# A hand-written order of work: the second batch's turns, and stages 2 and 3 of later batches, at other places

## The chip, the cores and the metric

The kernel runs on one core of a Trainium2 chip. The metric is the time of one execution on the device in microseconds (us); the median of several executions is compared. The core's engines are TensorE (PE in the profile; its weight loads are PEld), VectorE (DVE), ScalarE (ACT), GpSimd (POOL) and SyncE (SP), which here only issues transfers. Each engine works through its own instructions in the order in which the program gives them.

## The reference

Eight batches of 2496 positions and 256 channels go through a filter in the frequency domain, and each of the 19968 resulting rows then through one of eight experts, which is chosen by a hash of the row's token number.

```python
X = np.fft.rfft(x, axis=1)                       # x: (8, 2496, 256)
Y = X * (filt_r + 1j * filt_i)[None, :, :]
x = np.fft.irfft(Y, n=2496, axis=1).reshape(19968, 256)
expert_idx = token_ids * np.int64(2654435761) % np.int64(8)
for e in range(8):
    mask = expert_idx == e
    h = np.maximum(x[mask] @ w1[e], 0.0)         # w1: (8, 256, 1024)
    out[mask] = h @ w2[e]                        # w2: (8, 1024, 256)
```

All of it is in float32.

## The kernel before

**The filter.** 2496 is split as 39 x 64, and the transform of a batch is done in three stages. Stage 1 (`stage1`, or `stage1_c` for batches 0 and 1) is a transform over 39, with matmuls that write `pa`; stage 2 (`stage2`: `forward` writes `pb`, `back` writes `pc`) a transform over 64, the filter's product (three VectorE lines, 279 to 283, that make `y`) and the way back over 64; stage 3 (`stage3`, matmuls that write `pd`) the way back over 39. A batch has six pieces of stages 1 and 3 (`u` from 0 to 5; the last is smaller) and eleven of stage 2, since piece `u` does `forward(u)` and `back(u - 1)`.

Between the stages the layout changes. Batches 2 to 7 do that through DRAM: stage 1's result is stored to `d1` and loaded again by `load2`, stage 2's is stored to `d2` and loaded by `load4`. For batch 2 the stores of the later part of stage 1 are kept back (`put_off`) and issued from ScalarE's queue after `begin`. Batches 0 and 1 (`first`, `second`) stay on chip and are turned by TensorE: `turn2`, and `turn4(u)`, which transposes the columns of piece `u` into `pu` in two PSUM tiles (pools `xps` and `dps`, one buffer each), from which ScalarE (batch 0) or VectorE (batch 1) copies them to `t4`. One `t4` tile holds two pieces, and there are two such tiles. `stage3(u)` reads it.

**The rows.** `stage3` puts each finished row into a tile `o`, with the row's number in columns behind its 256 channels (line 378, on VectorE), and four columns of rows a piece are scattered by GpSimd with an indirect transfer each (`scatter`, line 391; 22 for a batch) to `xs` in DRAM, where rows of one expert lie together in tiles of 128. Batches 0 and 1 have four buffers for `o`, the others two.

**The experts.** The 159 tiles of 128 rows are worked on in steps. A step gathers the rows of a tile four steps ahead from `xs` (`load`, line 765), turns a tile (line 789), multiplies by `w1` (`up`, line 799, into `ups`; then ScalarE and VectorE make `ht` from it, lines 803 and 805), by `w2` (`down`, line 811, into `dps`), and scatters the result to `out` (line 815). Weights of an expert are loaded by SP two steps ahead (lines 422 and 425), under a condition that says whether the expert changes. The first 30 tiles hold only rows of batches 0 and 1, the next 40 only rows of batches up to 3, and so on; so experts can begin when batch 1 has been scattered, and the other batches are filtered in between.

**The order** is written out by hand. `todo` is a list of pairs of a number and a piece of work, sorted by the number. Pieces with a negative number come before the first step, in that order; a piece numbered `i + f` is put into step `i`: before `up` when `f` is under 0.5, otherwise between `up` and `down`. `spaced(t0, t1, n)` makes `n` evenly spaced numbers. `part1`, `part2` and `part3` give the numbers for stages 1, 2 and 3 of a batch and for its loads. The number only orders the program; engines wait for each other by semaphores. A transfer that has to wait for its data holds up all that SP, or GpSimd, is to issue after it.

Before the change the end of this first part is: `chain(21)`, then of batch 1 (B) and of batch 2's stage 1 (s1): B.turn4(0), B.stage3(0), B.turn4(1), s1(0), B.stage3(1), B.turn4(2), s1(1), three issues of weights and the fourth, B.stage3(2), B.turn4(3), B.stage3(3), B.turn4(4), B.stage3(4), B.turn4(5), B.stage3(5), s1(2) to s1(5), `begin` (which gathers for the first tiles), `put_off`, load2(0) to load2(3) of batch 2, load1(0) and load1(1) of batch 3. In step 0 stage2(0) of batch 2 follows `up`.

Of the kernel before, what the change touches and what calls it, by code (L numbers as in the profile page):

```python
# [30 lines left out]
H, HN = 3, 21  # L31
# [4 lines left out]
XG = 4  # L36
NU = (HN + XG) // XG
# [82 lines left out]
def kernel(  # L120
# [62 lines left out]
    class Batch:  # L183


        def __init__(self, b):
            self.b = b
            self.d1 = self.d2 = None
            self.x, self.t2, self.t4, self.p = {}, {}, {}, {}
            self.g = None  # L190
            if b < 2:

                own = mid[:, 5 * b:5 * b + 5, :].rearrange("p k f -> p (k f)")
                self.mixed = own.rearrange("p (h n s) -> p h n s", h=2, s=NS)
                after = (held[:, 0:NS * C] if b == 0 else mid[:, 0:5, :].rearrange("p k f -> p (k f)"))
                self.out = after.rearrange("p (h n s) -> p h n s", h=2, s=NS)
# [174 lines left out]
            for dram, chip in self.parts(self.d2, self.t4[v], v):  # L371
                nc.sync.dma_start(out=chip, in_=dram)

        def stage3(self, u):

            n = min(XG, HN + 1 - XG * u)
            o = (o2pool if self.b < 2 and u % 2 else opool).tile([NR, XG, W], F32, name=f"o_{self.b}_{u}", tag="o")
            nc.vector.tensor_scalar(o[:, 0:n, C:].bitcast(I32),
                                    tokno[:, XG * u:XG * u + n].unsqueeze(2).to_broadcast([NR, n, W - C]),
                                    float(self.b * S), None, op0=OP.add)  # L380
            v, half = divmod(u, XL // XG)

            copy = nc.scalar.copy if self.b < 2 else nc.vector.tensor_copy
            self.products(wi_t, (NK, 2 * NS), N1, self.t4[v][:, half * XG:half * XG + XG, :], o, copy, u, "pd")
            for i in range(n):
                j = XG * u + i
                r = NR if j < HN else N1
                scatter(o[0:r, i, :], sidx[0:r, self.b, j:j + 1], f"xs_{self.b}")

    def scatter(rows, index, group):  # L390
        st = nc.gpsimd.indirect_dma_start(  # L391
            out=xs[:], out_offset=bass.IndirectOffsetOnAxis(ap=index, axis=0),
            in_=rows, in_offset=None, bounds_check=NT * TB - 1, oob_is_err=False)
        for other in ["xs_pad", "xs_read"] + [f"xs_{b}" for b in range(B)]:
            tc.declare_no_dep(st.ins, group=other, reason="distinct rows")
        tc.add_to_no_dep_group(group, st.ins)

    batches = [Batch(b) for b in range(B)]
    first, second = batches[:2]
# [4 lines left out]
    def weights(i, which):  # L404

        if i >= NT:
            return
        if i >= 2 and which == 0:
            ws[i] = ws[i - 2][0:2]
        eng, kw = nc.sync, {}  # L410
        if which == 0:
            ws[i].append(eng.value_load(chunk_i[0:1, 0, i:i + 1], min_val=0, max_val=E - 1))
            if i >= 2:
                ws[i].append(eng.value_load(chunk_i[0:1, 1, i:i + 1], min_val=0, max_val=1))
        e = ws[i][2]
        if i >= 2:
            kw = {"cond": ws[i][3]}
        if which == 0:


            for f in (slice(0, F // 2), slice(F // 2, F)) if i < 2 else (slice(0, F),):
                eng.dma_start(out=ws[i][0][:, :, f],
                              in_=moe_w1[bass.ds(e, 1)].rearrange("one (p dp) f -> p (one dp) f", p=P)[:, :, f], **kw)
        else:
            eng.dma_start(out=ws[i][1], in_=moe_w2[bass.ds(e, 1)].rearrange("one (fp p) d -> p (one fp) d", p=P), **kw)
# [19 lines left out]
    def load_tables(part):  # L445
        if part < 2:

            nc.gpsimd.tensor_copy(junk[:], first.x[2 * part][0:1, 0, 0:1])
        sl = S_PARTS[part]
        nc.sync.dma_start(out=d_t[:, sl, :], in_=d_dram.ap()[:, sl, :])  # L450
        for k in range(2):
            load_filter(k, sl)
# [207 lines left out]
    def spaced(t0, t1, n):  # L660
        return [t0 + (t1 - t0) * u / n for u in range(n)]

    def part1(b, at, loads=None):
        bt = batches[b]
        if loads is None:

            loads = [at[2 * v] - 2.5 * (at[1] - at[0]) for v in range(NV)]
        return ([(at[u], lambda u=u: bt.stage1(u)) for u in range(NU)] +
                [(loads[v], lambda v=v: bt.load1(v)) for v in range(NV) if b > 0])

    def part2(b, at, ready):
        if isinstance(ready, list):
            bt = batches[b]
            return ([(at[u], lambda u=u: bt.stage2(u)) for u in range(NS // 2 + 1)] +
                    [(t, lambda g=g: bt.load2(g)) for g, t in enumerate(ready)])
        bt = batches[b]
        return ([(at[u], lambda u=u: bt.stage2(u)) for u in range(NS // 2 + 1)] +
                [(max(at[2 * g] - 4.5 * (at[1] - at[0]), ready), lambda g=g: bt.load2(g)) for g in range(NS // SG)])

    def part3(b, at, ready=None):  # L680
        bt = batches[b]
        if b < 2:
            return [(at[u], lambda u=u: bt.stage3(u)) for u in range(NU)]
        return ([(at[u], lambda u=u: bt.stage3(u)) for u in range(NU)] +
                [(max(at[2 * v] - 2.5 * (at[1] - at[0]), ready), lambda v=v: bt.load4(v)) for v in range(NV)])
# [4 lines left out]
    N_2 = NS // 2 + 1  # L690
# [8 lines left out]
    todo = [(t, lambda k=k: load_tables(k)) for k, t in enumerate((-160, -159, -157, -156))]  # L699
# [6 lines left out]
    todo += [(-150.4, lambda: first.turn2(0))]  # L706
    todo += [(t, lambda k=k: chain(k)) for k, t in enumerate(spaced(-150, -105, NS + 2))]
    todo += [(t, lambda u=u: second.stage1_c(u)) for u, t in enumerate(spaced(-147.5, -132, NU))]
    for bt, at in ((first, spaced(-123.7, -105, NU)), (second, spaced(-103, -85, NU))):
        todo += [(t - 2.6, lambda bt=bt, u=u: bt.turn4(u)) for u, t in enumerate(at)]  # L710
        todo += [(t, lambda bt=bt, u=u: bt.stage3(u)) for u, t in enumerate(at)]
    todo += [(-135, lambda: nc.sync.dma_start(out=wi_t[:], in_=wi_dram.ap()))]
    todo += [(t, lambda v=v: batches[2].load1(v)) for v, t in enumerate((-119, -117.5, -116))]
    todo += [(t, lambda u=u: batches[2].stage1(u)) for u, t in enumerate((-101.5, -99.5, -86, -85.5, -85, -84.5))]

    todo += [(-75.5, lambda: [nc.scalar.dma_start(out=dram, in_=chip) for dram, chip in put_off])]
    todo += [(t, lambda k=k: weights(k // 2, k % 2)) for k, t in enumerate((-99, -98.9, -98.8, -98.7))]
    todo += [(-76, lambda: begin())]

    todo += part1(3, spaced(1.5, 6.5, NU), [-74.6, -74.5, 2.5]) + part1(4, spaced(15, 20.5, NU))  # L720
    todo += part1(5, spaced(21, 27, NU)) + part1(6, spaced(35, 44.5, NU)) + part1(7, spaced(50, 60, NU))
    todo += part2(2, spaced(.55, 6, N_2), [-75, -74.9, -74.8, -74.7, 1.2]) + part2(3, spaced(9.2, 15.7, N_2), 6.6)
    todo += part2(4, spaced(22, 31, N_2), 20.5) + part2(5, spaced(31.2, 46, N_2), 28)
    todo += part2(6, spaced(48, 62, N_2), 47) + part2(7, spaced(63.2, 80, N_2), 61)
    todo += part3(2, spaced(8, 14.5, NU), 5.8) + part3(3, spaced(17, 25, NU), 15.6)
    todo += part3(4, spaced(33, 44, NU), 31.5) + part3(5, spaced(49, 63, NU), 46.5)
    todo += part3(6, spaced(67, 83, NU), 62) + part3(7, spaced(84, 101, NU), 81)
    todo.sort(key=lambda t: t[0])
# [7 lines left out]
    def begin():  # L736
        nonlocal gath, work, outs, nums
        rctx.close()
        gath, work, outs = pool(ctx, "gath", 4), pool(ctx, "work", 2), pool(ctx, "outs", 3)
        nums = pool(ctx, "nums", 4)  # L740
        for i in range(4):
            load(i)
# [3 lines left out]
    for o0, o in zip(np.cumsum([0] + [len(o) for o in order]), order):  # L746
        for i in range(len(o)):
            if o0 + i not in pair:
                n = next((j for j in (1, 2) if i + j < len(o) and abs(o[i + j] - o[i]) == 1
                          and o0 + i + j not in pair), 0)  # L750
# [142 lines left out]
```

## Time and profile before

| | us |
|---|---|
| median of 6 runs | 1528.28 (1519.88 to 1534.59) |
| the profiled execution | 1530.26 |
| its span, first to last instruction | 1528.5 |
| TensorE busy | 1463.7 |
| VectorE busy | 538.5 |
| ScalarE busy | 233.6 |
| GpSimd busy | 496.0 |
| start of the first `up` | 159.18 |

The profile gives for each instruction its line, its engine and the program's names of what it writes and reads (`pb<-mid,d_t`), and for the idle time before it who ended it. "remote" and "another core or an unknown queue" mean that the profile found no releaser of its own. A busy TensorE is not TensorE at its peak: its matmuls overlap, and the granted clock (a share of full speed) differs from stretch to stretch. About a tenth of the span lies ahead of the first `up`; from there on the steps run, about 7.0 us each where no filter work is in them (3.57 for `up`, 3.46 for `down`), and 10 to 12 in the first thirty.

### The profile page before, as it was taken

How to read it: one execution, taken by the hardware profiler on the slowest of the kernel's cores; microseconds unless marked ns; L12 is line 12 of the kernel's file. 1: busy time of each engine (PE TensorE's matmuls, PEld its weight loads, DVE VectorE, ACT ScalarE, POOL GpSimd, SP SyncE). 2: the span in 40 equal slices, each digit the busy share in tenths (PEclk: the TensorE clock that was granted, in tenths of full speed). 3: DMA queues.
4: the chain of work that ended last, by engine and by line, in shares of the span. 5: the costliest groups of instructions: out<-in, count | busy, mean ns of one | idle time of the engine just before them, and what ended most of it. 6: DMA issues, size and time to landing. Idle time of an engine off the chain costs nothing.

```text
span 1528.5 us, 25818 instructions
## 1 busy us (share of the span) xinstructions
PE 1463.7 (96%) x9340; PEld 1341.4 (88%) x9340; DVE 538.5 (35%) x1008; ACT 233.6 (15%) x401; POOL 496.0 (32%) x802
## 2 busy tenths in 40 slices
PE   6987799999999999989999999999999999999997
PEld 6875699888989988979899898899899999999996
DVE  5962353542444444244434343222221222222221
ACT  3652121111121111111101011000000000000000
POOL 6455023554432244224331343233312121211211
PEclk9998899999999999999999999999999999999999
DMA  8254668559875863765657442734331423132321
GB/s 221 58 196 133 189 217 205 192 196 252 252 216 161 231 198 108 213 173 150 197 135 213 149 132 79 203 115 130 99 100 35 148 76 107 42 97 83 102 85 28
DMA packets 186988, 226.06 MB, mean 148 GB/s; under 512 B 101653, under 2 KB 157389, under 8 KB 180890
## 3 DMA queue, kind: packets, MB, share of 16 engines
q1 hardware_dynamic: 154615, 146.92, 34.8%
q0 software_dynamic: 28096, 73.51, 14.7%
q10 hardware_dynamic: 4147, 3.94, 0.9%
q8 instruction: 76, 1.25, 0.3%
q14 instruction: 54, 0.44, 0.1%
HBM read 415.94 MB, written 75.08 MB: 321 GB/s over the span
## 4 chain that ended last, share of the span: by engine, by line
PE 87%; DMA 4%; another core or an unknown queue 2%; DVE 2%; issue 1%; SPq 1%; ACT 1%; ACTq 0%; POOL 0%; DVEq 0%
PE dps L811 35%; PE ups L799 35%; PE pd L228 4%; PE pb L273 4%; PE pc L295 3%; PE pa L228 3%; DMA wts<-in_x_dram 2%; DMA wts<-in_moe_w_dram 1%; DVE z L282 1%; DMA mid<-d 1%; PE pc L345 1%; DVE y L283 1%; PE pu L360 1%; DMA d<-mid 1%
## 5 line engine op out<-in xcount | busy, mean ns | idle before, releaser
L799 PEld LDWEIGHTS ups<-xt,wts 128*128 128x128 f32 x5088 | 594.3, 192 | 15.9 <-issue 7.4
L799 PE MATMUL ups<-xt,wts 128*128 128x128 f32 x5088 | 596.0, 276 | 5.0 <-issue 3.7
L811 PE MATMUL dps<-wts,ht 128*128 128x256 f32 x2544 | 581.2, 381 | 9.9 <-ACT ht L803 5.7
L811 PEld LDWEIGHTS dps<-wts,ht 128*128 128x128 f32 x2544 | 477.0, 191 | 75.0 <-ACT ht L803 6.7
L815 POOL DMA_INDIRECT out_dram<-osb,no x159 | 158.3, 995 | 557.0 <-DVE osb L814 460.5
L805 DVE TENSOR_SCALAR ht<-ups 128x512 f32<-128x512 f32 x159 | 110.0, 692 | 509.9 <-PE ups L799 447.2
L803 ACT ACTIVATE ht<-ups 128x512 f32<-128x512 f32 x159 | 94.9, 597 | 869.7 <-PE ups L799 746.7
L391 POOL DMA_INDIRECT xs<-o,sidx x176 | 176.7, 1004 | 107.6 <-issue 48.2
L814 DVE COPY osb<-dps 128x256 f32<-128x256 f32 x159 | 67.5, 425 | 355.8 <-PE dps L811 337.3
L782 POOL COPY no<-xg 32x2 int32<-32x2 int32 (+1 forms) x328 | 60.3, 184 | 278.4 <-DMA out_dram<-osb,no 183.8
L282 DVE TENSOR_TENSOR z<-pb,filt 64x512 f32<-64x512 f32 x160 | 110.2, 689 | 2.3
L228 PE MATMUL pd<-t,wi_t 120*117 120x256 f32 x320 | 78.6, 389 | 2.8 <-DVE t L364 2.6
L789 DVE STREAM_TRANSPOSE xt<-xg 128x256 f32<-128x256 f32 x159 | 69.1, 434 | 16.3 <-DMA d<-mid 16.3
L228 PEld LDWEIGHTS pd<-t,wi_t 120*117 120x117 f32 x320 | 57.9, 185 | 16.1 <-ACT o L230 2.8
L273 PE MATMUL pb<-mid,d_t 128*128 128x256 f32 x240 | 62.9, 385 | 9.0 <-DMA mid<-d 9.0
L279 DVE TENSOR_TENSOR y<-pb,filt 128x512 f32<-128x512 f32 x80 | 54.3, 679 | 47.7 <-PE pb L273 41.3
L298 ACT COPY mid<-pc 128x512 f32<-128x512 f32 x60 | 35.1, 585 | 232.2 <-PE pc L295 185.1
L283 DVE TENSOR_TENSOR y<-y,z 128x512 f32<-128x512 f32 x80 | 61.5, 769 | 2.7
L295 PE MATMUL pc<-y,e_t 128*128 128x256 f32 x240 | 61.7, 380 | 0.0
L228 PE MATMUL pa<-x,wf_t 117*120 117x256 f32 x224 | 55.2, 390 | 4.6 <-issue 4.5
L273 PEld LDWEIGHTS pb<-mid,d_t 128*128 128x128 f32 x240 | 43.8, 193 | 14.8 <-issue 6.6
L228 PEld LDWEIGHTS pa<-x,wf_t 117*120 117x120 f32 x224 | 41.2, 188 | 13.0 <-issue 5.3
(123 smaller groups left out, 560.7 us busy)
## 6 DMA issues: line engine op xcount, KB each, us to landing
wts<-in_moe_w_dram SPq DMA_DIRECT2D x320, 1024.0 KB
mid<-d SPq DMA_DIRECT2D x60, 256.0 KB
d<-mid POOLq DMA_DIRECT2D x60, 256.0 KB
xg<-xs SPq DMA_DIRECT2D x235, 64.0 KB
t<-d SPq DMA_DIRECT2D x12, 960.0 KB
x<-in_x_dram SPq DMA_DIRECT2D x36, 312.0 KB
d<-mid POOLq DMA_DIRECT2D x10, 960.0 KB
xg<-xs SPq DMA_DIRECT2D x77, 65.0 KB
```

Source lines behind the costliest of these rows:

```text
L228: nc.tensor.matmul(out=ps[0:cols * H, k, :], lhsT=w[:], rhs=src[:, 2 * i + k, :], start=True, stop=True)
L273: nc.tensor.matmul(out=ps[:, i, :], lhsT=d_t[:, s, :], rhs=rhs, start=True, stop=True)
L282: nc.vector.tensor_tensor(out=z[b], in0=ps[a], in1=f_t[1][a, sl, :], op=OP.mult)
L283: nc.vector.tensor_tensor(out=y[:], in0=y[:], in1=z[:], op=OP.add)
L295: nc.tensor.matmul(out=ps[:, i, :], lhsT=e_t[:, 2 * u + i, :], rhs=pr[:, i, :], start=True, stop=True)
L391: st = nc.gpsimd.indirect_dma_start(out=xs[:], out_offset=bass.IndirectOffsetOnAxis(ap=index, axis=0), in_=rows, in_offset=None, bounds_ch ...
L789: nc.vector.transpose(out=xt[i].rearrange("p d (a t) -> p a d t", t=32), in_=xg[i][0][:, 4 * xg[i][1]:4 * xg[i][1] + 4, 0:C // 4].rearrang ...
L799: nc.tensor.matmul(out=ps[:, k, :], lhsT=w1[:, dp, fp * P:(fp + 1) * P], rhs=xt[i][:, dp, :], start=(dp == 0), stop=(dp == DP - 1))
L803: nc.scalar.activation(out=dst, in_=ps[:], func=AF.Relu)
L805: nc.vector.tensor_scalar_max(dst, ps[:], 0.0)
L811: nc.tensor.matmul(out=ps[:, 0, :], lhsT=ht[:, fp, :], rhs=w2[:, fp, :], start=(fp == 0), stop=(fp == FP - 1))
L815: st = nc.gpsimd.indirect_dma_start(out=out[:], out_offset=bass.IndirectOffsetOnAxis(ap=to_rows[i], axis=0), in_=o[:], in_offset=None, bou ...
```

## The change

It writes the row numbers of `o` in a method of its own, `numbers3`, and calls it for the first four pieces of batch 0 long before their stage 3. It puts `turn4` of batch 1 two pieces ahead of `stage3`. It issues load1(0) and load1(1) of batch 3 ahead of batch 2's load2, and moves stages 2 and 3 of batches 2 and 3 and stage 1 of batch 3 to other numbers. Load2 of batch 6 may be issued from 46.3 on instead of 47.

```diff
-            self.x, self.t2, self.t4, self.p = {}, {}, {}, {}
+            self.x, self.t2, self.t4, self.p, self.o = {}, {}, {}, {}, {}
...
-        def stage3(self, u):
-
+        def numbers3(self, u):
             n = min(XG, HN + 1 - XG * u)
             o = (o2pool if self.b < 2 and u % 2 else opool).tile([NR, XG, W], F32, name=f"o_{self.b}_{u}", tag="o")
             nc.vector.tensor_scalar(o[:, 0:n, C:].bitcast(I32),
                                     tokno[:, XG * u:XG * u + n].unsqueeze(2).to_broadcast([NR, n, W - C]),
                                     float(self.b * S), None, op0=OP.add)
+            self.o[u] = o
+
+        def stage3(self, u):
+
+            n = min(XG, HN + 1 - XG * u)
+            if u not in self.o:
+                self.numbers3(u)
+            o = self.o[u]
...
-    for bt, at in ((first, spaced(-123.7, -105, NU)), (second, spaced(-103, -85, NU))):
-        todo += [(t - 2.6, lambda bt=bt, u=u: bt.turn4(u)) for u, t in enumerate(at)]
+
+    todo += [(-147.6, lambda u=u: first.numbers3(u)) for u in range(4)]
+
+    for bt, at, ahead in ((first, spaced(-123.7, -105, NU), 2.6), (second, spaced(-101, -86, NU), 5.1)):
+        todo += [(t - ahead, lambda bt=bt, u=u: bt.turn4(u)) for u, t in enumerate(at)]
...
-    todo += [(t, lambda u=u: batches[2].stage1(u)) for u, t in enumerate((-101.5, -99.5, -86, -85.5, -85, -84.5))]
+    todo += [(t, lambda u=u: batches[2].stage1(u)) for u, t in enumerate((-100.9, -98.4, -86, -85.5, -85, -84.5))]
...
-    todo += [(t, lambda k=k: weights(k // 2, k % 2)) for k, t in enumerate((-99, -98.9, -98.8, -98.7))]
+    todo += [(t, lambda k=k: weights(k // 2, k % 2)) for k, t in enumerate((-99, -98.9, -98.8, -98.3))]
...
-    todo += part1(3, spaced(1.5, 6.5, NU), [-74.6, -74.5, 2.5]) + part1(4, spaced(15, 20.5, NU))
+    todo += part1(3, spaced(2, 6.8, NU), [-75.3, -75.2, 3]) + part1(4, spaced(15, 20.5, NU))
...
-    todo += part2(2, spaced(.55, 6, N_2), [-75, -74.9, -74.8, -74.7, 1.2]) + part2(3, spaced(9.2, 15.7, N_2), 6.6)
+    todo += part2(2, spaced(1.6, 6.6, N_2), [-75, -74.9, -74.8, -74.7, 2.3]) + part2(3, spaced(9.4, 15.5, N_2), 6.6)
...
-    todo += part2(6, spaced(48, 62, N_2), 47) + part2(7, spaced(63.2, 80, N_2), 61)
-    todo += part3(2, spaced(8, 14.5, NU), 5.8) + part3(3, spaced(17, 25, NU), 15.6)
+    todo += part2(6, spaced(48, 62, N_2), 46.3) + part2(7, spaced(63.2, 80, N_2), 61)
+    todo += part3(2, spaced(8.55, 14.5, NU), 6.6) + part3(3, spaced(17.6, 25.1, NU), 16.2)
```

The order of batch 1's pieces after it, with the same short names: B.turn4(0), (1), (2), B.stage3(0), s1(0), three issues of weights, B.turn4(3), B.stage3(1), s1(1), the fourth issue of weights, B.turn4(4), B.stage3(2), B.turn4(5), B.stage3(3), (4), (5), s1(2) to s1(5). In the steps, batch 2's stage2(0) then follows `up` of step 1; step 2 has s1(0) of batch 3 and stage2(1) ahead of `up`, and stage2(2), s1(1) of batch 3 and stage2(3) between `up` and `down`. Load2(4) of batch 2 moves from step 1 to step 2, load1(2) of batch 3 from step 2 to step 3, and load4(0) of batch 2 from step 5 to step 6.

## The prediction

> **What bounds the kernel now.** I read the page first, then what TensorE waited for, then the chain of waits, then windows of two microseconds, then the timeline of the queues. In the page TensorE is busy nearly the whole span (first line: busy us, share, instructions); in its list of waits only a few are long (the rest: who waited for what, us in total, times, longest):
>
> ```profile
> PE 1463.7 (96%) x9340; PEld 1341.4 (88%) x9340; DVE 538.5 (35%) x1008; ACT 233.6 (15%) x401; POOL 496.0 (32%) x802
> PE pb L273 <- DMA mid<-d: 9.0, 2, 6.0
> PE dps L811 <- ACT ht L803: 5.7, 4, 2.6
> PE pu L360 <- ACT mid L347: 5.2, 1, 5.2
> ```
>
> Nothing but taking TensorE's waits away, or the slow matmuls behind them, can shorten the end. `pb L273` is stage 2, and its two waits are the ones the change aims at: 6.0 us in batch 2, 3.0 in batch 6. The chain of waits shows the first (start, length, what):
>
> ```profile
> 158.46 8.17 DMA d<-mid
> 167.38 3.11 DMA mid<-d
> 170.62 2.04 PE pb L273 x4
> 172.66 5.31 PE dps L811 x16
> ```
>
> Tile 0's `up` has ended (164.6), and TensorE stands until batch 2's put-off stores have landed and been loaded again. Afterwards its clock is at half (stretch, TensorE, weight loads, DVE, ACT, POOL, granted clock, DMA share, GB/s):
>
> ```profile
> 162.00:164.00 2.00, 2.00 (x17) 2.00 (x16) 0.00 (x0) 0.60 (x1) 0.00 (x0) 0.84 0.94 253
> 168.00:170.00 2.00, 0.00 (x0) 0.00 (x0) 0.00 (x0) 0.00 (x0) 0.00 (x0) 0.87 0.91 283
> 172.00:174.00 2.00, 2.00 (x6) 1.61 (x5) 1.28 (x2) 0.00 (x0) 0.00 (x0) 0.50 0.81 252
> 190.00:195.00 5.00, 5.00 (x31) 4.51 (x30) 3.19 (x5) 1.76 (x3) 1.49 (x2) 1.00 1.00 370
> ```
>
> The queues around it, from the timeline: POOL's first scatter of batch 1 and the hole in its train, ACT standing 5.78 us, SP's gathers, its loads for stage 2, and then the x of batch 3:
>
> ```profile
> 118.51 0.99 POOL L391 DMA_INDIRECT xs<-o,sidx  x1 [3.35 <-ACT o L230]
> 130.91 0.99 POOL L391 DMA_INDIRECT xs<-o,sidx  x1 [2.34 <-ACT o L230]
> 148.77 0.58 ACT L230 COPY mid<-pa 120x512 f32<-120x512 f32 x1 [5.78 <-issue]
> 150.48 1.82 SPq L765 DMA_DIRECT2D xg<-xs  x4
> 166.84 4.96 SPq L264 DMA_DIRECT2D mid<-d  x8
> 171.90 4.97 SPq L210 DMA_DIRECT2D x<-in_x_dram  x6
> ```
>
> SP is idle from 152.3 to 166.8.
>
> **Stage 2 of batch 2, from step 0 to step 1.** Before, from the start of tile 0's `up` (159.18) to that of tile 2 (193.47) is 34.3 us. At full clock its work is 23.6: two `up` of 3.57, two `down` of 3.46, four `pb` and three `pc` of 0.86, two stage 1 of 1.73 (all from the chain's later rows). The other 10.7 are 6.0 of waiting, and cold work: `up` 0 took 5.44 for 3.57, `pb` 2.04 for 0.86, `down` 0 5.31 for 3.46.
>
> After, stage2(0) stands behind tile 1's `up`. Let T be the start of `up` 0. TensorE reaches stage2(0) at T + 5.44 + 0.75 (waiting for DVE's `ht`, 164.62 to about 165.35) + 3.46 + 3.57 = T + 13.2. Its data landed at 170.6, which is T + 11.4. With no more than that, `up` 2 begins at T + 13.2 + 0.86 + 3.46 + 1.73 (stage1(0)) + 1.73 (stage2(1)) = T + 21.0. In step 2 then come 5.2 us that the old order had behind it (stage2(2), stage2(3), stage1(1)), so the old one counts as 34.3 - 5.2 = 29.1: **a gain of 8.1**. The weights for tile 2 don't stop it: both issues took about 0.1 us (182.81, 183.41) where a real load took 0.38 to 0.42, and the byte rate falls after them, so I read them as skipped; SP, without the 5.0 us of x in front, reaches them at about 176 to 179 instead of 182.8.
>
> **x of batch 3 ahead of those loads.** Six loads of 312 KB go into SP's idle stretch, behind the gathers and ahead of stage 2's loads. SP doesn't pay: 5.0 us of issuing from 152.3, plus a wait for stage1(5) (its TensorE work ended at 155.5), is over before 166.8. The DMA engines may: ACT's put-off stores (960 + 600 + 40 KB) took 8.17 us at a DMA share of 0.94. If no byte of x meets them, the delay c is 0. If all 1.87 MB do, at the stores' own rate of 1.6 MB in 8.17 us, c is 9.5. The windows from 152 to 158 have shares of 0.48, 0 and 0.32, so I let the first half of x pass there, and charge the other 0.94 MB at 250 GB/s: **c = 3.7**. stage2(0) begins at T + 11.4 + 3.7 = T + 15.1, 1.9 later than TensorE gets there, and the gain is **6.2** (0.5 with c = 9.5).
>
> [...]
>
> **Turns of batch 1 two pieces ahead.** Before: turn 0 (ended 115.54), product 0. After: turns 0, 1, 2, product 0. Each turn needs two PSUM tiles that DVE's copies (1.29 to 1.48 us a pair) free, so product 0 starts after two pairs, at about 118.1 instead of 115.54; at warm clock (1.89 for 3.31) its second copy ends some 2.4 us later and the first scatter is at 120.9. POOL's train is 22 x 1.29 = 28.4 us, end about 149.0. Before it ended at 148.63, with a hole of 2.0. So the later start is paid by the hole, if two pieces of lead close it; if not, +2.4. Further on TensorE no longer waits for each turn's copy, so batch 2's stage 1 comes earlier, under POOL's train. ACT's part of the first gathers was issued at 155.90, behind stage 1's last copies, 5.4 us after SP's part. If ACT is ready, both go at about 151, and T is 154.5 instead of 159.18: 4.7 gained. If its standstill recurs behind the later train, T is 2.4 later. ACT's stop at 143.0 to 148.8 had no data dependency I can name, so I stay near the middle of the two ends: **1.4 gained**. Stores and loads follow ACT and so T; c stays.
>
> **Numbers early.** Four DVE writes of 0.18 us move to about 46 us, where DVE is the busiest (36.7 of 38 us in the window 38 to 76) and TensorE later waits for its `y`: **0.7 lost**, from 0 to 0.7. The gain is nothing: the first scatter (80.07, after 14.49 waiting for DVE `o L378`) could start at 77.6, but that of piece 3 at 100.24 waits for ACT's copy (ended 100.0), and batch 1 starts behind TensorE anyway. Without that cover it would be worth the 2.4.
>
> **Batch 6, loads at 46.3 for 47.** SP issued them at 648.63 and took 7.22 us for six; `pb` waited 2.95 (656.00). A step earlier is 7.0 us earlier, and their source was stored at 613.0: **2.9 gained**, between 0 (weights that then queue behind) and 2.95.
>
> **The other moves** of stages 2 and 3 of batches 2 and 3 by up to one step: TensorE is busy 40 of 40 us from 190 to 230 and from 230 to 270, so the same work in another order costs nothing while its data is there. Batch 3's last scatter ran at 432.2, the gather that needs it about 450.9: half a step later (some 5 us) is covered by that 18.
>
> **Sum.** 6.2 + 1.4 - 0.7 + 2.9 = 9.8 us. The profiled execution took 1530.26 (span 1528.5, 1.8 around it), 2.0 over the median of 1528.28: 1520.5 for it, **1518.5 for the median**. Best ends: 8.1 + 4.7 + 2.95 = 15.8, 1512.5. Worst: 0.5 - 2.4 - 0.7 = 2.6 lost, 1530.9.
>
> [...]
>
> **Rivals.**
> 1. *The x loads take the engines.* c = 9.5, stage 2 of batch 2 waits as long as before, one step later: 0.5 + 2.9 - 0.7 = 2.7 gained, **1525.6**; with the other small terms at their lower ends, no change. For it: the share of 0.94. Against it: the idle 152 to 158.
> 2. *Slower: TensorE's results are released late, and the new order has less queued behind them.* At 277.6 ACT and DVE stood 6.65 and 5.45 us with their inputs computed, and TensorE then waited 2.62 and ran `down` in 5.41 for 3.46: 4.6 us. The same happened at 344.3 (ACT 5.16, DVE 10.41). Before, the other such stops fell where TensorE had other work. The new step 2 holds three pieces in one half and steps 0 and 1 almost none. From three more such stops in steps 1 to 11 on (13.8 against 9.8) the kernel is slower than before; with four, **1537**. Against it: DVE's chain of 2.8 us still has 3.5 us of TensorE work to hide behind.
> 3. *The turns ahead only delay POOL* (T + 2.4, hole not closed, ACT as late): 6.2 - 2.4 + 2.9 - 0.7 = 6.0, **1522.3**.
>
> **How the numbers follow.** A measurement of this kernel can tell 0.5% from no change, 7.6 us: faster is under 1520.6, slower over 1535.9. Forecast 0.58 (its own range 1512 to 1521), rival 1 0.14, rival 3 0.12, rival 2 0.16. The forecast's upper edge falls into "same", and as much of rival 3 into "faster". So faster 0.60, same 0.24, slower 0.16. The range, 1509 to 1533, holds the forecast, rivals 1 and 3 and the spread of a median (runs before: 1519.9 to 1534.6), and leaves out rival 2 and little else.
>
> **What would show it.** Right: no wait of `pb L273` over 2 us in batch 2, `down` 0 at 3.5 us, x loads issued before 160, `up` 0 to `up` 2 about 23 us; batch 6's wait of 2.95 gone; a first scatter near 121 and no hole in the train. Wrong: stores landing more than 12 us after their issue (rival 1), new waits of `dps L811` on ACT or DVE `ht` between 170 and 300 (rival 2), ACT's gathers still 5 us behind SP's (rival 3).

## The result, and the profile after

The changed kernel took 1520.51 us (median of 20 runs, 1516.12 to 1524.22), the kernel before beside it 1528.61 (46 runs): a ratio of 0.9947 [0.9935, 0.9959], or 8.1 us faster. The profiled execution took 1521.24 us with a span of 1519.5, against 1530.26 and 1528.5. In the new file `up` is line 809, `down` 821, `ht` 813 and 815, the gathers 775, the kept-back stores 726, the scatter of rows 398; 210, 264 and 273 are as before.

The first two lines are of the page (busy us, share, instructions; then the granted clock in 40 slices of 38 us), the others of the list of what TensorE waited for (us in total, times, longest).

```profile
PE 1463.0 (96%) x9340; PEld 1340.4 (88%) x9340; DVE 537.8 (35%) x1008; ACT 233.3 (15%) x401; POOL 497.1 (33%) x802
PEclk9997799999999999999999999999999999999999
```

```profile
PE pb L273 <- DMA mid<-d: 4.0, 1, 4.0
PE dps L821 <- ACT ht L813: 3.6, 3, 1.8
PE pu L360 <- ACT mid L347: 1.6, 1, 1.6
PE pd L228 <- DMA t<-d: 1.1, 1, 1.1
```

The two waits of stage 2 were 9.0 us together, now it is one of 4.0; batch 6's is gone. The two sevens in the clock line are the slices from 114 to 190 us; before, these two digits were 8, so the slow stretch around the first steps is not gone. The chain of waits (start, length, what) has the place:

```profile
159.91 13.47 DMA d<-mid
174.01 3.15 DMA mid<-d
177.29 2.04 PE pb L273 x4
179.33 5.13 PE dps L821 x16
```

The kept-back stores now take 13.47 us instead of 8.17, and what follows the wait is again slow: 2.04 for a `pb` of 0.86, 5.13 for a `down` of 3.46. Windows of two microseconds (stretch, TensorE, weight loads, DVE, ACT, POOL, granted clock, DMA share, GB/s) show why:

```profile
175.00:177.00 2.00, 0.00 (x0) 0.00 (x0) 0.00 (x0) 0.00 (x0) 0.00 (x0) 0.69 0.83 274
177.00:179.00 2.00, 1.71 (x4) 1.47 (x5) 0.00 (x0) 0.00 (x0) 0.00 (x0) 0.50 0.84 272
181.00:183.00 2.00, 2.00 (x7) 1.58 (x6) 1.16 (x2) 0.00 (x0) 0.00 (x0) 0.60 1.07 290
183.00:185.00 2.00, 2.00 (x11) 1.74 (x10) 0.42 (x1) 0.00 (x0) 0.00 (x0) 1.00 0.43 80
```

The clock falls in the wait and is back only after 183. The queues, from the timeline (start, length, engine, line, what; in brackets the idle time before it and who ended it):

```profile
120.03 0.99 POOL L398 DMA_INDIRECT xs<-o,sidx  x1 [6.53 <-ACT o L230]
131.68 0.99 POOL L398 DMA_INDIRECT xs<-o,sidx  x1 [1.58 <-ACT o L230]
151.04 0.58 ACT L230 COPY mid<-pa 120x512 f32<-120x512 f32 x1 [5.09 <-remote]
151.26 1.82 SPq L775 DMA_DIRECT2D xg<-xs  x4
153.22 13.39 SPq L210 DMA_DIRECT2D x<-in_x_dram  x6
155.91 2.37 ACTq L775 DMA_DIRECT2D xg<-xs  x4
158.88 3.04 ACTq L726 DMA_DIRECT2D d<-mid  x3
173.46 4.97 SPq L264 DMA_DIRECT2D mid<-d  x8
639.47 3.73 SPq L264 DMA_DIRECT2D mid<-d  x4
648.69 1.03 PE L273 MATMUL pb<-mid,d_t 128*128 128x256 f32 x4
```

The x loads are issued in SP's once idle stretch, but take 13.4 us there, beside the stores: from 158 to 172 us the packets of ACT's queue took 55.5% of the time of the 16 DMA engines, those of SP's 22.5%. POOL's train of scatters begins 1.5 us later and still has a hole. ACT stands 5.09 us as it stood 5.78, and issues its gathers 4.7 us behind SP's. Batch 6's loads are issued 9 us earlier (639.47 for 648.63; 4 us of that because the whole run is ahead by then), and its stage 2 has no idle time ahead of it.

Where the 9.0 us of the two profiled executions come from is read from the start of `up` of chosen tiles (the last columns: tile 2 to tile 25, tile 47 to 48, and from there to the end of the run). Experiments are in it too, by set, for later use; each set ran on a chip of its own.

| profiled run | total | `up` 0 | `up` 2 | 0 to 2 | 2 to 25 | 47 to 48 | rest |
|---|---|---|---|---|---|---|---|
| before | 1530.3 | 159.2 | 193.5 | 34.3 | 249.4 | 11.1 | 873.3 |
| after | 1521.2 | 159.7 | 187.8 | 28.1 | 251.7 | 7.9 | 871.7 |
| first set: b6_only | 1505.3 | 146.1 | 179.8 | 33.7 | 248.3 | 7.9 | 867.0 |
| steps_only | 1506.1 | 146.3 | 174.2 | 28.0 | 250.1 | 11.2 | 867.9 |
| x_behind | 1506.5 | 150.1 | 178.8 | 28.6 | 250.0 | 7.9 | 867.7 |
| prologue_only | 1510.6 | 149.4 | 183.2 | 33.8 | 248.5 | 9.6 | 867.1 |
| second set: after_again | 1512.9 | 152.3 | 181.4 | 29.0 | 250.5 | 7.9 | 870.7 |
| no_turns | 1509.0 | 154.3 | 178.2 | 23.9 | 250.3 | 7.9 | 870.4 |
| no_numbers | 1518.0 | 155.9 | 184.4 | 28.6 | 250.3 | 7.9 | 872.1 |
| stores_first | 1515.4 | 164.0 | 185.2 | 21.2 | 250.6 | 7.9 | 869.5 |
| third set: no_turns_2 | 1514.8 | 153.5 | 182.5 | 29.0 | 250.7 | 7.9 | 871.4 |
| no_turns_x_behind | 1515.5 | 155.8 | 184.0 | 28.2 | 251.4 | 7.9 | 869.9 |
| sp_gathers | 1511.2 | 153.1 | 181.4 | 28.4 | 251.1 | 7.9 | 868.3 |
| sp_gathers_x0 | 1508.5 | 157.6 | 177.9 | 20.3 | 250.7 | 7.9 | 869.9 |

The old order has 5.2 us of work ahead of `up` 2 that the new one has behind it, so before's columns are to be read as 29.1 and 254.6. Then the change lost 0.5 up to `up` 0, gained 1.0 to `up` 2, 2.9 to `up` 25, 0.8 to `up` 47, 3.2 at batch 6 and 1.6 behind it: 9.0. Between `up` 25 and 47 and behind `up` 48 the change moves no work, so 2.4 of the 9.0 belong to no part of it. The stretch behind `up` 48 differs by 2.5 us among the four profiles of the second set too (869.5 to 872.1).

### The profile page after: what moved, and what is told of

Its sections match the earlier page's. It is cut to its first block, busy times and chain, and to the rows that moved or that the text cites. A ratio compares the mean times of both kernels' runs of the same rounds, so it can differ in the third digit from the quotient of the medians.

```text
span 1519.5 us, 25802 instructions
## 1 busy us (share of the span) xinstructions
PE 1463.0 (96%) x9340; PEld 1340.4 (88%) x9340; DVE 537.8 (35%) x1008; ACT 233.3 (15%) x401; POOL 497.1 (33%) x802
## 3 DMA queue, kind: packets, MB, share of 16 engines
q0 software_dynamic: 28096, 73.51, 15.1%
## 4 chain that ended last, share of the span: by engine, by line
PE 90%; DMA 5%; issue 1%; DVE 1%; another core or an unknown queue 1%; ACT 0%; SPq 0%; ACTq 0%; DVEq 0%
PE ups L809 35%; PE dps L821 35%; PE pd L228 4%; PE pb L273 4%; PE pa L228 3%; PE pc L295 3%; DMA wts<-in_x_dram 1%; PE pc L345 1%; DMA d<-mid 1%; DMA wts<-in_moe_w_dram 1%; DMA d_t<-d_tbl 1%; PE pa L324 1%; PE pu L360 1%; PE pt L334 1%
## 5 line engine op out<-in xcount | busy, mean ns | idle before, releaser
L228 PE MATMUL pa<-x,wf_t 117*120 117x256 f32 x224 | 58.7, 405 | 6.8 <-issue 6.7
L228 PEld LDWEIGHTS pa<-x,wf_t 117*120 117x120 f32 x224 | 42.3, 194 | 17.6 <-issue 10.5
```

What stands on the lines that cost most here:

```text
L228: nc.tensor.matmul(out=ps[0:cols * H, k, :], lhsT=w[:], rhs=src[:, 2 * i + k, :], start=True, stop=True)
```

## The experiments

Every set had runs of the kernel before beside it: 1508.66 us in the first, 1519.85 in the second, 1521.22 in the third. Gains in us are differences of medians within a set; a bracket behind one is the ratio's interval times the median of the kernel before.

**b6_only**: the kernel before with batch 6's loads alone moved.

```diff
-    todo += part2(6, spaced(48, 62, N_2), 47) + part2(7, ...)
+    todo += part2(6, spaced(48, 62, N_2), 46.3) + part2(7, ...)
```

> The kernel before with one number changed: load2 of batch 6 from 46.3 on. My theory: the wait of pb L273 at 656 (2.95 us) goes and nothing takes its place, so 2.5 to 3.5 us faster (ratio 0.998), the same in the profile from about 650 on. Rival: weights that are now queued behind it cost as much, 0 us.

Measured: 1506.75, ratio 0.9992 [0.9983, 1.0001], 1.9 us gained (-0.2 to 2.6; the ratio alone says 1.2). In the profile the step from tile 47 to 48 takes 7.9 us against 11.2 and 9.6 in the two runs of this set that load at 47. The mechanism is as expected, worth 1.7 to 3.3 there; by the times it is not told apart from nothing. This run also serves as the old order of this chip. From its timeline, with no standstill of ACT, and its chain at stage 3 of batch 3:

```profile
112.14 0.99 POOL L391 DMA_INDIRECT xs<-o,sidx  x1 [0.52 <-ACT o L230]
139.30 0.90 POOL L391 DMA_INDIRECT xs<-o,sidx  x1 [0.30 <-issue]
146.12 6.04 PE L799 MATMUL ups<-xt,wts 128*128 128x128 f32 x28 [10.21 <-DVE xt L789]
```

```profile
327.73 11.45 DMA t<-d
339.32 3.58 PE pd L228 x8
```

POOL's train starts at 112.1 and has hardly a hole to its end at 139.3 plus 0.9; tile 0 begins 6.8 us after the last scatter's start. Stage 3 of batch 3 waits for its load (4.0 us in the list of waits) and then runs cold, 3.58 for 1.73.

**steps_only**: the kernel before with the moves of stages 1, 2 and 3 of batches 2 and 3; x stays behind load2.

```diff
-    todo += part1(3, spaced(1.5, 6.5, NU), [-74.6, -74.5, 2.5]) + ...
+    todo += part1(3, spaced(2, 6.8, NU), [-74.6, -74.5, 3]) + ...
-    todo += part2(2, spaced(.55, 6, N_2), [..., 1.2]) + part2(3, spaced(9.2, 15.7, N_2), 6.6)
+    todo += part2(2, spaced(1.6, 6.6, N_2), [..., 2.3]) + part2(3, spaced(9.4, 15.5, N_2), 6.6)
-    todo += part3(2, spaced(8, 14.5, NU), 5.8) + part3(3, spaced(17, 25, NU), 15.6)
+    todo += part3(2, spaced(8.55, 14.5, NU), 6.6) + part3(3, spaced(17.6, 25.1, NU), 16.2)
```

> The kernel before with the moves of stages 2 and 3 of batches 2 and 3 and of stage 1 of batch 3 alone; x of batch 3 stays behind load2, the turns and numbers stay, batch 6 stays. My theory: in the changed kernel the step was worth only 1.0 us because x, loaded ahead, stretched the put-off stores from 8.2 to 13.5 us. Here they take 8 to 9 us again, stage2(0) waits under 1 us, and from up 0 to up 2 it is 21 to 23 us instead of 28.1: 5 to 8 us faster than before (ratio 0.995 to 0.9965). Rival: x, now behind load2, is late for batch 3's stage 1 in step 2, TensorE waits there for as long, and the gain is 0 to 2 us.

Measured: 1502.74, 0.9962 [0.9948, 0.9975], 5.9 us gained (3.8 to 7.8). The time is the expected one, but not for the expected reason. The chain, at the two places that matter:

```profile
160.56 8.35 DMA x<-in_x_dram
169.04 3.57 PE pa L228 x8
...
331.03 9.66 DMA t<-d
340.73 1.99 PE pd L228 x8
```

Stage 2 of batch 2 waits no more, since the stores land as fast as before: from ACT's first issue of them to SP's first load of stage 2 it is 8.89 us in both (144.81 to 153.70, and 157.95 to 166.84 before). But stage 1 of batch 3, right behind it, waits 4.8 us for x and runs cold (3.57 for 1.73): `up` 0 to `up` 2 takes 28.0 us, much as in the changed kernel. **The wait went from one load to the next.** What this edit did gain lies behind it. Stage 3 of batch 3, which starts 0.6 of a step later, waits 2.3 instead of 4.0 and runs at 1.99 instead of 3.58; from `up` 2 to `up` 25 it is 250.1 against 253.5 (248.3 + 5.2), 3.4 us. The two other profiles of this set agree: that wait is 4.2 in prologue_only (old numbers) and 2.2 in x_behind (new ones).

**x_behind**: the changed kernel, x of batch 3 behind load2 as before.

```diff
-    todo += part1(3, spaced(2, 6.8, NU), [-75.3, -75.2, 3]) + ...
+    todo += part1(3, spaced(2, 6.8, NU), [-74.6, -74.5, 3]) + ...
```

> The changed kernel with load1(0) and load1(1) of batch 3 behind load2 again. My theory: put-off stores 8 to 9 us for 13.5, stage2(0) waits under 1 us for 4.0 and the cold work behind it (2.9 us) goes: 5 to 7 us faster than the changed kernel, ratio to before 0.990 to 0.992. Rival: the same wait comes back at batch 3's stage 1, whose x lands late: 0.9947 as the changed kernel, or over it.

Measured: 1504.67, 0.9969 [0.9953, 0.9985], 4.0 us gained (2.3 to 7.1). Stage 1 of batch 3 waited 6.4 us for x, as the rival said; the expected 0.990 to 0.992 was not reached. The gain agrees with the sum of its three parts in this set: 5.9 (steps) + 1.9 (batch 6) - 4.0 (the next run) = 3.8, though by the ratios it is 2.8 against 4.7, and each part is uncertain by 1 to 2 us. The changed kernel was not run on this chip; elsewhere its ratio was 0.9947 and 0.9968, so it is not shown that x ahead helps the changed kernel itself.

**prologue_only**: the kernel before with the changed first part alone (turns two ahead, numbers early, stage 1 of batch 2 and the weights at their new numbers).

```diff
-    for bt, at in ((first, spaced(-123.7, -105, NU)), (second, spaced(-103, -85, NU))):
-        todo += [(t - 2.6, lambda bt=bt, u=u: bt.turn4(u)) for u, t in enumerate(at)]
+    todo += [(-147.6, lambda u=u: first.numbers3(u)) for u in range(4)]
+    for bt, at, ahead in ((first, spaced(-123.7, -105, NU), 2.6), (second, spaced(-101, -86, NU), 5.1)):
+        todo += [(t - ahead, lambda bt=bt, u=u: bt.turn4(u)) for u, t in enumerate(at)]
...
-    todo += [... enumerate((-101.5, -99.5, -86, -85.5, -85, -84.5))]
+    todo += [... enumerate((-100.9, -98.4, -86, -85.5, -85, -84.5))]
...
-    todo += [... enumerate((-99, -98.9, -98.8, -98.7))]
+    todo += [... enumerate((-99, -98.9, -98.8, -98.3))]
```

> The kernel before with the turns two pieces ahead, batch 2's first two pieces of stage 1 and the fourth issue of weights moved with them, and the numbers early, and nothing else. My theory: up 0 starts within 1.5 us of before (159.2), since ACT's gathers still go out at about 156, and the time is the same within 2 us (ratio 0.9987 to 1.0013). Rival: the turns ahead gave the 3 to 4 us of the changed kernel that neither the loads of batch 6 nor stage 2 of batch 2 account for (ratio 0.9975).

Measured: 1512.65, 1.0027 [1.0016, 1.0037]: **4.0 us slower** (2.4 to 5.6), outside what was expected and outside its rival. The timeline of its POOL and its first `up`:

```profile
115.25 0.98 POOL L398 DMA_INDIRECT xs<-o,sidx  x1 [3.22 <-ACT o L230]
142.45 0.90 POOL L398 DMA_INDIRECT xs<-o,sidx  x1 [0.30 <-issue]
149.44 2.90 PE L809 MATMUL ups<-xt,wts 128*128 128x128 f32 x12 [12.90 <-DVE xt L799]
```

Against b6_only the train starts 3.1 us later, ends 3.2 later, and `up` 0 starts 3.3 later. On this chip the train had no hole that two pieces of lead could close, so what the two extra turns put ahead of the first product was lost. (The numbers written early are in this run too; no run on this chip has the turns alone.)

**after_again**: the changed kernel as it is, on the second chip, for the next ones.

> The changed kernel once more, to stand beside the next three on one chip. The first four runs were on a chip where TensorE's results are not released late (no stop of 5 us of ACT with its inputs ready) and where the kernel before takes 1508.7 us. My theory: the change is the sum of its parts, prologue +4.1, steps -5.7, batch 6 -1.2, so on such a chip 2 to 4 us faster, ratio 0.998; the 8.1 us of the first measurement need a chip with late releases. Rival: the gain doesn't depend on that, ratio 0.9947 anywhere.

Measured: 1515.03, 0.9968 [0.9949, 0.9987], 4.8 us faster than before (2.0 to 7.8). `pb` waited 5.8 us. From its chain, to set beside the next run:

```profile
152.33 14.44 DMA d<-mid
172.76 5.30 PE dps L821 x16
```

**no_turns**: the changed kernel with batch 1's turns one piece ahead, as before.

```diff
-    ... (second, spaced(-101, -86, NU), 5.1)):
+    ... (second, spaced(-103, -85, NU), 2.6)):
-    todo += [... enumerate((-100.9, -98.4, -86, -85.5, -85, -84.5))]
+    todo += [... enumerate((-101.5, -99.5, -86, -85.5, -85, -84.5))]
-    todo += [... enumerate((-99, -98.9, -98.8, -98.3))]
+    todo += [... enumerate((-99, -98.9, -98.8, -98.7))]
```

> The changed kernel with batch 1's turns one piece ahead, as before; the numbers stay early and all else stays changed. My theory: the first scatter of batch 1 and up 0 are 3 to 4 us earlier where results aren't released late, and the time is 2.5 to 4 us under that of the changed kernel on the same chip (ratio to before 0.995 to 0.996). On a chip with late releases 0 to 2 us over it. Rival: the early start is lost again at the wait of stage2(0), because the stores set it; then no difference from the changed kernel.

Measured: 1510.02, 0.9930 [0.9906, 0.9954]: 9.8 us faster than before, 5.0 faster than the changed kernel beside it; the slowest of its six runs (1511.98) is under the fastest of the changed kernel's twelve (1512.57). On this chip the change is better without its turns two pieces ahead. The profiles put the difference at another place than in the set before. `up` 0 is not earlier but 2.0 later (154.3 against 152.3), and from `up` 2 on no_turns is 3.1 ahead. Its chain:

```profile
154.36 12.06 DMA d<-mid
170.38 1.10 PE pb L273 x4
171.48 3.45 PE dps L821 x16
```

The stores land at 166.4, in after_again at 166.8, although they were issued 2.0 us later here; so TensorE waits 3.1 instead of 5.8, and `pb` and `down` come at 1.10 and 3.45 instead of 2.04 and 5.30. Windows of the same stretch (columns as above):

```profile
167.00:169.00 2.00, 0.27 (x3) 0.08 (x1) 1.04 (x2) 0.00 (x0) 0.72 (x4) 1.00 0.57 154
169.00:171.00 2.00, 0.62 (x3) 0.60 (x4) 0.00 (x0) 0.00 (x0) 0.00 (x0) 1.00 0.82 285
```

The clock stays at 1.00 through a wait of 3.1. That pair of profiles differs by 3.9 us in all, and 3.1 of it is here.

**no_numbers**: the changed kernel with all numbers in `stage3`.

```diff
-    todo += [(-147.6, lambda u=u: first.numbers3(u)) for u in range(4)]
```

> The changed kernel with the numbers of batch 0 written in stage 3 as before. My theory: the first scatter is 2 to 3 us later, that of batch 1 is not, and the time is that of the changed kernel within 1 us. Rival (my prediction): 0.7 us faster than it, because four DVE writes leave the stretch where DVE is fullest.

Measured: 1515.84, 0.9962 [0.9945, 0.9979], with the changed kernel beside it at 1515.03. The numbers early change nothing that these runs can tell; a gain or loss of 3 us stays possible.

**stores_first**: an attempt at something better. steps_only and b6_only together, x behind load2, and ACT issues the kept-back stores ahead of its first gathers.

```diff
-    todo += [(-75.5, lambda: [nc.scalar.dma_start(out=dram, in_=chip) for dram, chip in put_off])]
+    todo += [(-76.5, lambda: [nc.scalar.dma_start(out=dram, in_=chip) for dram, chip in put_off])]
```

> The kernel before with the steps' moves and batch 6's, x of batch 3 behind load2, and batch 2's put-off stores issued by ACT ahead of the first gathers instead of behind them. My theory: what stage 2 of batch 2 and stage 1 of batch 3 wait for is 5.6 MB of stores, loads and x that all go through the DMA engines after the gathers. With 1.6 MB of it in the time in which ACT and the engines wait for POOL's scatters, neither waits, up 0 to up 2 takes 21 to 22.5 us for 27.9, and the time is 9 to 13 us under before (ratio 0.9915 to 0.994). Rival: the gathers lie behind the stores on the same engines and up 0 is later by 4 us or more: ratio 0.997 or over. On a chip with late releases ACT's stage 1 ends at 155.8, the gathers behind it come 3 us later, and the gain is that much smaller.

Measured: 1511.26, 0.9935 [0.9910, 0.9960], 8.6 us faster than before. Its timeline:

```profile
152.63 1.82 SPq L765 DMA_DIRECT2D xg<-xs  x4
154.25 2.52 ACTq L716 DMA_DIRECT2D d<-mid  x2
157.40 4.47 ACTq L765 DMA_DIRECT2D xg<-xs  x4
163.98 6.59 PE L799 MATMUL ups<-xt,wts 128*128 128x128 f32 x32 [10.25 <-issue]
177.44 1.03 PE L273 MATMUL pb<-mid,d_t 128*128 128x256 f32 x4
```

There is no wait of stage 2 or stage 1 left: 21.2 us from `up` 0 to `up` 2, the 21.0 of the prediction's undisturbed sum. But ACT's gathers stand behind its stores and take 4.47 us to issue, and `up` 0 moves to 164.0. The wait went ahead of the first step. This execution took 1515.43, the slowest of the six and 4.2 over the median, so `up` 0 need not be as late in the others.

**no_turns_2**: no_turns again, on a third chip, beside the next three.

> The kernel of no_turns once more, to stand beside the next three on one chip: ratio to before 0.993 (0.991 to 0.9955), as there; it is the changed kernel with batch 1's turns one piece ahead.

Measured: 1512.01, 0.9933 [0.9917, 0.9949], the same ratio as in the second set. This time the profiled execution (2.75 us over the median) had the long wait, 6.4 us, and 29.0 us from `up` 0 to `up` 2.

**no_turns_x_behind**: no_turns with x behind load2 (the edit of x_behind).

> no_turns with x of batch 3 behind load2, as before the change. My theory: the DMA engines have the same bytes to move before batch 3's stage 1, so the wait goes from stage2(0) (there 3 us) to stage 1 of batch 3 (4 to 5 us): the same as no_turns within 2 us, and the place of x's loads is worth little either way. Rival: the x loads ahead are what made the step pay, 4 us or more slower than no_turns. Other rival (from my prediction, c costs 1.9 us and more): 3 us or more faster.

Measured: 1515.85, 0.9965 [0.9953, 0.9978]: **x ahead is worth 3.8 us** by the medians, in the order without the turns ahead. The chain:

```profile
168.04 0.88 PE pb L273 x4
...
170.51 7.84 DMA x<-in_x_dram
178.48 3.74 PE pa L228 x8
```

As in steps_only: stage 2 does not wait, stage 1 of batch 3 waits 6.1 us for x and runs cold. The time lies between the expectation (within 2 us) and its rival (4 us or more). Where the 3.8 us arise the profiles don't show: that of no_turns_2, with its wait of 6.4, is only 0.8 us shorter in all, and longer from `up` 0 to `up` 2 (29.0 against 28.2).

**sp_gathers**: stores_first, with all first gathers on SP, so that ACT's stores need not stand ahead of any.

```diff
-            ld = (nc.scalar if i < 2 and q % 2 else nc.sync).dma_start(
+            ld = nc.sync.dma_start(
```

> The kernel of stores_first (steps' and batch 6's moves, put-off stores ahead of the first gathers) with all of the first gathers issued by SP. My theory: in stores_first the step took the 21.2 us that it should, but up 0 came at 164.0, because ACT's gathers were issued behind the stores at 157.4 to 161.4. With SP issuing all eight behind the last scatter, up 0 starts 5 to 8 us earlier, the step still takes 21 to 24 us: ratio to before 0.987 to 0.991, the fastest so far. Rival: the stores hold the gathers up on the engines whoever issues them, up 0 at 162 or later, 0.9935 as stores_first.

Measured: 1510.37, 0.9931 [0.9913, 0.9948]. `up` 0 is at 153.1 and stage 2 waits 1.4, but stage 1 of batch 3 waits 5.7. Its x was issued behind stage 2's loads, from 166.60 to 171.57. That x is late again is inferred, for the list of waits names a gather issued behind x as what ended the wait. The expected 0.987 to 0.991 was not reached.

**sp_gathers_x0**: the same with only load1(0) of batch 3, three of the six x loads, ahead of load2.

```diff
-    todo += part1(3, spaced(2, 6.8, NU), [-74.6, -74.5, 3]) + ...
+    todo += part1(3, spaced(2, 6.8, NU), [-75.3, -74.5, 3]) + ...
```

> sp_gathers with load1(0) of batch 3 ahead of load2 (load1(1) stays behind). My theory: SP and the engines have room between the gathers and load2, stage 1 of batch 3 in step 2 doesn't wait for x: 1 to 3 us faster than sp_gathers. Rival: it delays load2 by as much as it saves: the same within 1 us.

Measured: 1508.10, 0.9919 [0.9897, 0.9941], the lowest ratio of all, 13.1 us faster than before. The timeline:

```profile
148.39 7.97 SPq L765 DMA_DIRECT2D xg<-xs  x8
150.60 2.28 ACTq L716 DMA_DIRECT2D d<-mid  x2
156.79 2.60 SPq L210 DMA_DIRECT2D x<-in_x_dram  x3
157.58 5.65 PE L799 MATMUL ups<-xt,wts 128*128 128x128 f32 x32 [8.18 <-issue]
```

TensorE waits for neither load, and `up` 0 to `up` 2 takes 20.3. SP needs 7.97 us to issue eight gathers beside ACT's stores, where four took 1.82 alone (in stores_first), so `up` 0 is later again. In sp_gathers, where ACT issued its stores 2 us later, the eight took 3.79. The edit touches nothing ahead of them, so this difference is one between executions. The interval of sp_gathers_x0 overlaps those of sp_gathers and no_turns_2, and the changed kernel was not run beside it; that it beats the kernel before is shown, that it beats the changed kernel only by ratios from different chips (0.9919 against 0.9947 and 0.9968).

## Why the prediction was right, and where it was not

The sum said 9.8 us and the profile has 9.0, the times 8.1. That agreement is partly luck: two terms were too large, and a term that had been put at nothing, together with 2.4 us in stretches that the change leaves alone, filled them up. Of the signs that were named beforehand, two that speak for rivals came (stores landing 13.47 us after their issue, ACT's gathers 4.7 us behind SP's), and for stage 2's step the one of the forecast did not (28.1 us from `up` 0 to `up` 2, not about 23).

- **The step of stage 2, forecast 6.2, measured 1.0.** The order works as described: TensorE reaches stage 2 at `up` 0 + 13.6 (forecast 13.2). Two things of the working were mis-sized. The delay c by the x loads was 5.3 us (13.47 against 8.17), not 3.7, and the stores started 1.0 later against `up` 0; so stage 2 began at `up` 0 + 17.6 instead of 15.1. And the wait of 1.9 was taken as a wait only. It became 4.0, and the work behind it ran cold: 1.18 more for `pb` and 1.67 more for `down`. 2.5 + 2.9 is the 5.2 that is missing, within 0.2. Rival 1's price of 0.5 for this step (0.4 by its own numbers) was nearer than the forecast's.
- **What both the forecast and rival 1 missed** is that x cannot simply be left behind either. steps_only and no_turns_x_behind take the x loads away from the stores, and the same wait appears at stage 1 of batch 3, 4.8 and 6.1 us long with cold work behind it. Within this stretch the engines have to carry the stores (1.6 MB), stage 2's loads and x (1.87 MB) whatever the order. Putting x ahead fills time in which they were idle: from 152 to 158 the DMA shares were 0.48, 0 and 0.32 before and are 0.55, 0.55 and 0.79 in the changed kernel. It is worth 3.8 us by the medians of no_turns_2 and no_turns_x_behind. That the filled time is the cause is argued, not shown. The stores took 5.3 us longer beside the x loads (13.47 against 8.17); that loading ahead loses did not follow from it.
- **Turns two pieces ahead, forecast 1.4 gained, measured a loss.** In the profile of the change `up` 0 came 0.5 later: the train began at 120.03 (forecast 120.9), its hole shrank only from 2.34 to 1.58, and ACT's gathers were as late as before. That is rival 3. Its price is larger than the 2.4 it was given: 4.0 us in prologue_only (with the numbers early), where the later `up` 0 is seen, and 5.0 by the medians of no_turns, where it is not. In the second set the profiles show the difference at the wait of stage 2. How the turns cause that is open: there is one profile a kernel, and the wait was 6.4 in the third set's no_turns, with the same ratio.
- **Batch 6, forecast 2.9:** 3.2 in the profile. Alone, by the times, 1.9 (-0.2 to 2.6).
- **The other moves, forecast 0, gave about 3 us.** "The same work in another order costs nothing while its data is there" failed at its condition. On the first set's chip stage 3 of batch 3 stood for its load, with the cold matmuls behind it, and starting it at 17.6 instead of 17 brought 3.4 us. In the first pair of profiles the gain in this stretch looks different, and it is not shown that the moves caused it: before, `down` waited 2.62 and 2.00 us for `ht` between tiles 2 and 25 and ran once at 5.41 for 3.46, 6.6 in all; after, there are waits of 1.02, 1.14 and 1.38 and 0.5 of slower work behind them, 4.1. That is 2.5 of the 2.9.
- **Numbers early, forecast 0.7 lost:** no_numbers cannot tell it from 0.
- **Rival 2, slower:** ACT's standstill ahead of the steps is still there (5.09 at 151.04), but from step 2 to 25 TensorE waited less for `ht` than before, as just counted, not more.

Not tried: the changed kernel beside x_behind on one chip, the turns ahead without the early numbers on the first set's chip, and no_turns with half of x ahead.

## What to carry to other kernels

In these runs, giving one load the earlier place moved the wait to the other: stage 2 waited 3.1 to 6.4 us with all of x ahead, stage 1 of batch 3 4.8 to 6.4 with x behind. Where a load moved ahead gains, the likely reason is that its bytes go into time in which the DMA engines were idle. So look for idle engine time first (here 152 to 158 us, where three windows had DMA shares of 0.48, 0 and 0.32), and count the bytes up to the next two consumers, not only to the one that waits. When you price a wait of TensorE, price the cold matmuls behind it as well: here a wait of 4.0 us cost 6.9. And do not put more in front of the first item of a queue that is itself the bound, as GpSimd's 22 scatters were (in prologue_only they began 3.1 us later than in b6_only, and `up` 0 came 3.3 later), unless the queue has holes to give back.

## What the runs showed of the hardware

The cost of a wait is not smooth. After 3.1 us without matmuls (no_turns) the granted clock was 1.00 and `down` took 3.45; after 4.0 (the changed kernel) it was 0.50 and `down` took 5.13. But the length of a wait alone does not decide. From the kernel before (two lines of the timeline, with a window between them, columns as above):

```profile
284.88 5.41 PE L811 MATMUL dps<-wts,ht 128*128 128x256 f32 x16 [2.62 <-ACT ht L803]
287.00:289.00 2.00, 2.00 (x6) 1.62 (x5) 1.13 (x2) 0.00 (x0) 0.00 (x0) 0.52 0.03 8
656.00 1.13 PE L273 MATMUL pb<-mid,d_t 128*128 128x256 f32 x4 [2.95 <-DMA mid<-d]
```

A wait of 2.62 us was followed by a clock of 0.52 and a `down` of 5.41, while one of 2.95 left the clock at 1.00 (window 655 to 657). Longer waits behind the first `up` were followed by a clock of 0.50 (6.0 us in the kernel before, 4.0 in the changed one, 6.1 in no_turns_x_behind) or by slow matmuls: stage 3 of 3.58 for 1.73 after 4.0 in b6_only, stage 1 of 3.57 for 1.73 after 4.8 in steps_only, a `pb` of 2.04 for 0.86 after 5.8 in after_again and 6.4 in no_turns_2. Of the three waits of 2.62, 2.95 and 3.1 us, one was followed by a halved clock and two were not. So the clock of 1.00 after no_turns' 3.1 may not come again.

The kernel before took 1528.61, 1508.66, 1519.85 and 1521.22 us in the four series of measurements, a spread of 1.3% that is larger than the change; the last three are on three chips. A part of it is ahead of the first `up`: 159.2 us in the first profile, 146.1 in b6_only. In the first, ScalarE stands 5.78 us (in the changed kernel 5.09) with its matmul done by the profile; in the first set's profiles no such stop was found (1.68 us at most from 128 to 137 us in b6_only and steps_only). Why it stands there in one series and not in another is open. The changed kernel's gain was 8.1 us in one series and 4.8 in another, with intervals of the ratio that overlap (0.9935 to 0.9959 and 0.9949 to 0.9987). So a difference of a few microseconds was only read between kernels that ran on one chip.
